# Two multiplies of the decay norm on GpSimd instead of VectorE, from block 3 on

## The chip, the cores and the metric

The kernel runs on one core of a Trainium2 chip. The core has a matrix engine (TensorE, PE in the profile), three engines for elementwise work (VectorE or DVE, ScalarE or ACT, GpSimd or POOL), an engine that issues transfers (SyncE or SP) and 16 DMA engines. Every engine runs its own list of instructions in order and waits on semaphores for the others. The metric is the device time of one execution in microseconds. The kernel before takes 1702.69 us, the median of three runs (1702.55 to 1706.17).

## The reference

A linear attention with complex, data-dependent decays feeds a mixture of eight experts whose gates are balanced by eight Sinkhorn steps. Shapes: batch 4, 8 heads, 768 steps, head size 48; 3072 tokens of 384 features; expert width 1024.

```python
mag = np.sqrt(a_re * a_re + a_im * a_im)
scale = np.minimum(mag, 0.999) / (mag + 1e-06)
a_re_n, a_im_n = (a_re * scale, a_im * scale)
for t in range(S):
    S_re, S_im = decay(S_re, S_im; a_re_n[t], a_im_n[t]) + (k[t] v[t], 0)
    y[t] = q[t] . S_re
x = y as 3072 x 384
P = sinkhorn(exp(x @ w_gate - max), 8 rounds)
out = sum over e of P[:, e] * (relu(x @ w1[e]) @ w2[e])
```

(The loop over t is shortened here.) The change touches the third line alone: the two products of a decay's real and imaginary part with its scale.

## The kernel before

The tokens are cut into 12 blocks of 256 (two batch entries by 128 steps). The first stage, about the first 550 us, goes through the blocks, and for each of them does the following.

- `norm`: loads the decays z (128 partitions, real and imaginary part, 768 columns each), works out the scale on ScalarE and VectorE, and multiplies both parts by it. The factor lies in the tile tx; L438 (L436 in the first two blocks) writes it last, and L440 makes the two products, in place in z. z has two buffers, z_236 and z_237, used by even and odd blocks.
- `scan`: forms the products of the decays over the steps of a chunk, on VectorE (L467 to L473), in place in z.
- `post`: from these the scaled keys kh (L511 to L526) and the scaled queries, in place in z (L530).
- `attention`: SyncE's queue moves kh and z to the tiles ks and qs (L558), TensorE makes the scores (L602), VectorE masks them into sc (L605), TensorE forms the output (L627), and ScalarE and VectorE split it into a high part xh and a low part xl (L642, L643), the x of the block. ScalarE and VectorE also carry the state on (L656 to L666).
- `experts`: experts 0 and 1 on the x of the block before. For each of their 8 column blocks TensorE makes nine matmuls of the first layer (L267 to L269, into ph), ScalarE the relu as hh and hf (L273), VectorE the difference hl (L277), and TensorE six matmuls of the second layer (L285 to L287, into po).

The rest of the time, from about 565 us, TensorE works through experts 2 to 7 by a scheme with fewer products (L1277 to L1279 and L1356 to L1358).

The order of instructions in the first stage is not that of the code. Each piece of work is put down as a job with an engine, a duration that the author supposes, the tiles that it reads and writes, and a rank. `Plan.order` then plays these jobs through: at each point the engine that can start first takes, of its jobs that are ready, the one with the lowest rank. The order that comes out is written into the program for every engine, TensorE's too. So a job's supposed duration moves the instructions of other engines as well. GpSimd had no jobs in this plan; its memsets stand where the code calls for them.

The norm of block i + 1 is put down ahead of the end of block i, and its jobs have ranks that let them run while block i is finished. For the block index i the jobs of L427 to L440 belong to the norm of block i.

Of the kernel before, what the change touches and what calls it, by code (L numbers as in the profile page):

```python
# [10 lines left out]
ALU = mybir.AluOpType  # L11
# [5 lines left out]
E, F = 8, 1024  # L17
# [43 lines left out]
class Plan:  # L61
# [20 lines left out]
    def order(self):  # L82
        n = len(self.ops)
        left = [len(o[5]) for o in self.ops]
        users = [[] for _ in range(n)]
        for k, o in enumerate(self.ops):
            for d in o[5]:
                users[d].append(k)
        ready = [0.0] * n
        self.start, self.end = [None] * n, [None] * n  # L90
        free = {e: 0.0 for e in ("PE", "DVE", "ACT", "SP")}
        queue = {e: [] for e in free}
        for k in range(n):
            if not left[k]:
                queue[self.ops[k][0]].append(k)
        out, pipe = [], 0.0
        while any(queue.values()):
            best = None
            for e, q in queue.items():
                if q:  # L100
                    t = max(free[e], min(ready[k] for k in q))
                    if best is None or t < best[0]:
                        best = (t, e)
            t, e = best
            k = min((k for k in queue[e] if ready[k] <= t + (0.12 if 0 <= self.ops[k][3] < 2000 else 0.35 if -9.6e5 < self.ops[k][3] <= -9e5 else 0.0)), key=lambda k: (self.ops[k][3], k))
            queue[e].remove(k)
            eng, us, run, rank, land, deps, kb, slack = self.ops[k]
            t = max(t, ready[k])
            self.start[k] = t
            free[e] = t + us  # L110
            end = t + (land or us)
            if kb:
                pipe = max(pipe, t + 1.0) + kb / 300.0
                end = max(end, pipe + 1.0)
            self.end[k] = end
            out.append(k)
            for u in users[k]:
                r = end + ((1.2 if self.ops[u][0] == "PE" else 0.2) if land else self.REACH.get((e, self.ops[u][0]), 0.15)) + slack
                ready[u] = max(ready[u], r)
                left[u] -= 1  # L120
                if not left[u]:
                    queue[self.ops[u][0]].append(u)
        assert len(out) == n
        return out


class Net:
# [188 lines left out]
    def phase1(self, c1, ca):  # L316
        tc, nc = self.tc, self.nc
# [68 lines left out]
        self.opening(K)  # L386
        order = self.plan.order()
        n = 1 + max(k for k, o in enumerate(order) if o not in self.expert and o not in self.late)
        assert not self.late & set(order[:n])
        E_ = mybir.EngineType  # L390
        with tc.manual_schedule(engines={E_.DVE, E_.Activation, E_.SP}):
            for k in order[:n]:
                self.plan.ops[k][2]()
        self.rest = [self.plan.ops[k][2] for k in order[n:]]
# [7 lines left out]
    def norm(self, i):  # L402
        nc, V, A, job = self.nc, self.nc.vector, self.nc.scalar, self.plan.add
        s, fl, ns = i % 2, self.fl, self.N // SUB
        zt = self.zt[s]
        zn = [("z", s, a, g) for a in range(2) for g in range(NCT * NCH)]
        R = 1000 * i
        if i == 0:
            for k in (0, 3):
                for a in range(2):  # L410
                    job("SP" if a else "ACT", 0.45, lambda a=a, k=k: (nc.sync if a else nc.scalar).dma_start(zt[:, a, k:k + 3, :CH], self.aqk[0, :, a, k:k + 3]), (), [("z", s, a, g) for g in range(k, k + 3)], -2e6 + k, land=3.0, kb=192)
        else:
            job("SP", 0.45, lambda: nc.sync.dma_start(zt[:, :, :, :CH], self.aqk[i, :, 0:2]), (), zn, -1.82e6 if i == 1 else -1e5, land=8.5, kb=768)
        for k, ps in enumerate([range(3), range(3, 6)] if i == 0 else [range(6)]):
            def nm(*t):
                return [(*t, g) for g in ps]

            n, ga, gb = CH * len(ps), ps[0], ps[-1] + 1
            z, sq = zt[:, :, ga:gb, :CH], self.sq[:, :, ga:gb]
            x, y, zz = (t[:, ga:gb] for t in (self.tx, self.ty, self.tz))  # L420
            zs = [("z", s, a, g) for a in range(2) for g in ps]
            X, Y, Z = nm("tx"), nm("ty"), nm("tz")
            f0, f1 = (i, ns + i) if k == 0 else (2 * ns + ns * NCT * NCH, 2 * ns + ns * NCT * NCH + 1)
            r = R - 1001 if i > 2 else R - 401 if i == 2 else R - 90 if i else R - 300 + 20 * k
            u = 900 if i > 2 else 0
            job("ACT", n / 522 + 0.1, lambda z=z, sq=sq, f0=f0: A.activation(sq, z, AF.Square, accum_out=fl[:, f0:f0 + 1]), zs, Y + Z, r - 5e5)
            job("DVE", n / 960 + 0.105, lambda sq=sq, x=x: V.scalar_tensor_tensor(x, sq[:, 0], 1e-20, sq[:, 1], ALU.max, ALU.add), Y + Z, X, r)  # L427
            job("ACT", n / 1045, lambda x=x, y=y: A.activation(y, x, AF.Abs_reciprocal_sqrt), X, Y, r + 1 - 5e5)
            job("ACT", n / 1045 + 0.1, lambda y=y, zz=zz, f1=f1: A.activation(zz, y, AF.Square, accum_out=fl[:, f1:f1 + 1]), Y, Z, r + 2 - 5e5)
            job("DVE", n / 960 + 0.075, lambda x=x, zz=zz: V.tensor_tensor(x, x, zz, ALU.mult), X + Z, X, r + 0.1)  # L430
            job("DVE", n / 960 + 0.105, lambda x=x, y=y: V.scalar_tensor_tensor(y, x, -3.0, y, ALU.add, ALU.mult), X + Y, Y, r + 4)
            job("ACT", n / 830, lambda y=y, zz=zz: A.activation(zz, y, AF.Square, bias=self.bm05[:, :1], scale=-0.5e-6), Y, Z, r + 5 - 5e5)
            if i < FOLD:
                job("DVE", n / 1920 + 0.087, lambda x=x, y=y: V.tensor_scalar(x, y, -0.4995, 1.0, ALU.mult, ALU.min), Y, X, r + 6)
                job("DVE", n / 960 + 0.105, lambda x=x, zz=zz: V.scalar_tensor_tensor(x, zz, 0.75, x, ALU.add, ALU.mult), X + Z, X, r + 7 + u)
            else:  # L436
                job("ACT", n / 1045, lambda zz=zz: A.activation(zz, zz, AF.Identity, bias=self.bw[:, :1], scale=-0.4995), Z, Z, r + 6 - 5e5)
                job("DVE", n / 960 + 0.105, lambda x=x, y=y, zz=zz: V.scalar_tensor_tensor(x, y, -1 / 0.4995, zz, ALU.max, ALU.mult), Y + Z, X, r + 7 + u)  # L438
            for a in range(2):
                job("DVE", n / 960 + 0.075, lambda z=z, x=x, a=a: V.tensor_tensor(z[:, a], z[:, a], x, ALU.mult), X + zs[a * len(ps):(a + 1) * len(ps)], zs[a * len(ps):(a + 1) * len(ps)], r + 8 + a + u)  # L440

    def scan(self, i):
        V, job = self.nc.vector, self.plan.add
# [1182 lines left out]
```

## Time and profile before

| | |
|---|---|
| median of three runs | 1702.69 us |
| span of the profiled execution | 1699.2 us, 3.5 us less than the median |
| TensorE busy | 1672.3 us (98%) |
| VectorE busy | 1281.3 us (75%) |
| ScalarE busy | 803.1 us (47%) |
| GpSimd busy | 8.9 us (1%) |

The span runs from the first to the last instruction on the core; the execution also has some time around it, which the runs' times hold and the span doesn't. Busy times are unions: two matmuls that overlap in TensorE's pipeline count once. The mean duration of a matmul (334 ns for 384 columns, say) is longer than the distance between two of them, since they overlap. GpSimd's 20 instructions are all memsets.

### The profile page before, as it was taken

To read this page: it belongs to the slowest core of one execution; us is meant where nothing else is said; L and a number is where in the kernel's file an instruction comes from. 1 tells how busy PE (TensorE), PEld (TensorE's weight loads), DVE (VectorE), ACT (ScalarE), POOL (GpSimd) and SP (SyncE) were. 2 spreads that over 40 slices of the span, in tenths; PEclk is the share of its full clock that TensorE was granted. 3 is DMA by queue.
4 is the path that set the end of the run, shared out by engine and by line. 5 is a ranking of instruction groups with operands and counts; after the bars stand their busy time and mean duration, and the time that the engine had idled before them with its cause. 6 is when DMAs were issued, how large, how long until landed. Compare 5 with 4: busy or idle time off the path is not lost.

```text
span 1699.2 us, 35042 instructions
## 1 busy us (share of the span) xinstructions
PE 1672.3 (98%) x13776; PEld 1631.4 (96%) x13776; DVE 1281.3 (75%) x2942; ACT 803.1 (47%) x1866; POOL 8.9 (1%) x20
## 2 busy tenths in 40 slices
PE   6999999999999999999999999999999999999998
PEld 3899999999999999999999999999999999999998
DVE  8899989999994989999854767665566766465665
ACT  7766656656553655555543333333333333333332
POOL 1000000000000000000000000000000000000000
PEclk9999999999999999999999999999999999999999
DMA  7445555445545888788875565666465566555460
GB/s 228 124 116 136 125 131 130 118 118 131 130 105 151 261 320 299 272 277 293 305 263 215 198 229 193 257 239 240 178 224 204 214 250 222 211 193 211 183 245 35
DMA packets 163469, 338.79 MB, mean 199 GB/s; under 512 B 14880, under 2 KB 122848, under 8 KB 163296
## 3 DMA queue, kind: packets, MB, share of 16 engines
q1 hardware_dynamic: 162496, 336.08, 59.0%
q8 instruction: 110, 1.80, 0.4%
q14 instruction: 63, 0.52, 0.1%
q10 hardware_dynamic: 800, 0.39, 0.1%
HBM read 236.27 MB, written 81.20 MB: 187 GB/s over the span
## 4 chain that ended last, share of the span: by engine, by line


## 5 line engine op out<-in xcount | busy, mean ns | idle before, releaser
L1376 ACT ACTIVATE hh<-s 128x384 fp32r<-128x384 f32 x378 | 198.9, 526 | 413.7 <-DVE s L1372 373.2
L1372 DVE TENSOR_TENSOR s<-s,A 128x384 f32<-128x384 f32 x315 | 174.0, 552 | 139.5 <-PE A L1358 137.0
L1279 PE MATMUL po<-w_d,hl 128*128 128x384 f32 x768 | 256.6, 334 | 0.0
L1278 PE MATMUL po<-w_d,hh 128*128 128x384 f32 x768 | 256.6, 334 | 0.0
L1277 PE MATMUL po<-w_d,hh 128*128 128x384 f32 x768 | 256.6, 334 | 0.0
L1383 DVE SCALAR_TENSOR_TENSOR hl<-s,hh 128x384 fp32r<-128x384 f32 x378 | 208.7, 552 | 6.1
L267 PE MATMUL ph<-xh,w 128*128 128x256 f32 x576 | 165.7, 288 | 1.2 <-ACT hl L273 0.8
L269 PE MATMUL ph<-xh,w 128*128 128x256 f32 x576 | 162.3, 282 | 0.0
L268 PE MATMUL ph<-xl,w 128*128 128x256 f32 x576 | 162.2, 282 | 0.0
L1369 ACT ACTIVATE s<-B 128x384 f32<-128x384 f32 x189 | 92.9, 491 | 117.7 <-PE B L1358 114.4
L1372 DVE TENSOR_TENSOR s<-s,B 128x384 f32<-128x384 f32 x189 | 104.1, 551 | 53.9 <-PE B L1358 51.6
L1277 PEld LDWEIGHTS po<-w_d,hh 128*128 128x128 f32 x768 | 144.2, 188 | 0.0
L1278 PEld LDWEIGHTS po<-w_d,hh 128*128 128x128 f32 x768 | 144.2, 188 | 0.0
L1279 PEld LDWEIGHTS po<-w_d,hl 128*128 128x128 f32 x768 | 144.2, 188 | 0.0
L273 ACT ACTIVATE hh<-ph 128x256 fp32r<-128x256 f32 x192 | 73.5, 383 | 131.2 <-PE ph L269 130.7
L285 PE MATMUL po<-w,hh 128*128 128x384 f32 x384 | 131.6, 343 | 0.0
L286 PE MATMUL po<-w,hh 128*128 128x384 f32 x384 | 128.9, 336 | 0.0
L287 PE MATMUL po<-w,hl 128*128 128x384 f32 x384 | 128.8, 336 | 0.0
L1279 PE MATMUL po<-w_c,hl 128*128 128x384 f32 x384 | 128.3, 334 | 0.0
L1278 PE MATMUL po<-w_c,hh 128*128 128x384 f32 x384 | 128.3, 334 | 0.0
L1277 PE MATMUL po<-w_c,hh 128*128 128x384 f32 x384 | 128.3, 334 | 0.0
L1391 DVE TENSOR_TENSOR s<-s,B 128x384 f32<-128x384 f32 x63 | 34.9, 554 | 115.7 <-PE B L1358 115.7
(258 smaller groups left out, 4075.7 us busy)
## 6 DMA issues: line engine op xcount, KB each, us to landing
w_d<-w_d SPq DMA_DIRECT2D x64, 768.0 KB, 7.2
w_a<-w_d SPq DMA_DIRECT2D x48, 768.0 KB, 4.3
w_b<-w_d SPq DMA_DIRECT2D x48, 768.0 KB, 5.7
w_c<-w_d SPq DMA_DIRECT2D x48, 768.0 KB, 6.3
raw<-in_w_dram SPq DMA_DIRECT2D x32, 576.0 KB, 5.8
w_d<-w_a SPq DMA_DIRECT2D x16, 768.0 KB, 3.2
w_d<-w_b SPq DMA_DIRECT2D x16, 768.0 KB, 5.0
w_d<-w_c SPq DMA_DIRECT2D x16, 768.0 KB, 6.3
```

What stands on the lines that cost most here:

```text
L267: nc.tensor.matmul(p, w[:, 0, cs], xh[:, ct, :], start=(ct == 0), stop=False)
L268: nc.tensor.matmul(p, w[:, 0, cs], xl[:, ct, :], start=False, stop=False)
L269: nc.tensor.matmul(p, w[:, 1, cs], xh[:, ct, :], start=False, stop=(ct == NCT - 1))
L285: nc.tensor.matmul(o, hh[:, s], w2h, start=f == 0, stop=False)
L286: nc.tensor.matmul(o, hh[:, s], w2l, start=False, stop=False)
L287: nc.tensor.matmul(o, hl[:, s], w2h, start=False, stop=f == NF - 1)
L1277: nc.tensor.matmul(po[k], hh[:, s], w2[:, 0], start=c == 0, stop=False)
L1278: nc.tensor.matmul(po[k], hh[:, s], w2[:, 1], start=False, stop=False)
L1279: nc.tensor.matmul(po[k], hl[:, s], w2[:, 0], start=False, stop=c == NF - 1)
L1372: V.tensor_tensor(S[nm], S[nm], ps, op)
L1376: A.activation(hh, S[nm], AF.Relu)
L1383: V.scalar_tensor_tensor(hl, S[nm], 0.0, hh.bitcast(F32), ALU.max, ALU.subtract)
```

## The change

For blocks 3 to 11 the two multiplies of L440 become jobs of GpSimd, with a supposed duration of n/400 + 0.2 us, which is 2.12 us for n = 768, in place of n/960 + 0.075. For that the plan gets a fifth engine, and the scheduler of the surrounding framework is told that GpSimd's order is given too. Blocks 0 to 2 stay as they were.

```diff
-        free = {e: 0.0 for e in ("PE", "DVE", "ACT", "SP")}
+        free = {e: 0.0 for e in ("PE", "DVE", "ACT", "SP", "POOL")}
...
-        with tc.manual_schedule(engines={E_.DVE, E_.Activation, E_.SP}):
+        with tc.manual_schedule(engines={E_.DVE, E_.Activation, E_.SP, E_.Pool}):
             for k in order[:n]:
                 self.plan.ops[k][2]()
...
             for a in range(2):
-                job("DVE", n / 960 + 0.075, lambda z=z, x=x, a=a: V.tensor_tensor(z[:, a], z[:, a], x, ALU.mult), X + zs[a * len(ps):(a + 1) * len(ps)], zs[a * len(ps):(a + 1) * len(ps)], r + 8 + a + u)
+                job("POOL" if i > 2 else "DVE", n / 400 + 0.2 if i > 2 else n / 960 + 0.075, lambda z=z, x=x, a=a, E=nc.gpsimd if i > 2 else V: E.tensor_tensor(z[:, a], z[:, a], x, ALU.mult), X + zs[a * len(ps):(a + 1) * len(ps)], zs[a * len(ps):(a + 1) * len(ps)], r + 8 + a + u)
```

The instructions move as follows. On GpSimd the 18 multiplies stand in pairs behind the memsets of block 1 (L631), with one row of another kind ahead of them. The end of its list before, and the same place now:

```order
L631 MEMSET st_222 128x512
L631 MEMSET st_223 128x512
L841 MEMSET lt_8469 128x384
L841 MEMSET lt_8502 128x384
```

```order
L631 MEMSET st_222 128x512
L631 MEMSET st_223 128x512
L440 ISA
L440 TENSOR_TENSOR z_237<-z_237,tx 128x6x128 x2
L440 TENSOR_TENSOR z_236<-z_236,tx 128x6x128 x2
```

Nothing else on GpSimd moved; the other seven pairs follow in the same way, even and odd buffers in turn.

On VectorE the place is the norm of block 10, whose buffer is z_236; hl_8_n are the differences of the experts on block 8, and L530 ends block 9. Before:

```order
L438 SCALAR_TENSOR_TENSOR tx<-sq 128x768
L440 TENSOR_TENSOR z_236<-z_236,tx 128x6x128
L277 TENSOR_TENSOR hl_8_1_6535<-hf_8_1_6517,hh_8_1_6470 128x256
L512 SCALAR_TENSOR_TENSOR ta<-kh 128x768
L277 TENSOR_TENSOR hl_8_2_6554<-hf_8_2_6541,hh_8_2_6537 128x256
L440 TENSOR_TENSOR z_236<-z_236,tx 128x6x128
L517 TENSOR_TENSOR kh<-ta,tb 128x768
```

Now:

```order
L530 TENSOR_TENSOR z_237<-z_237,qk 128x6x128
L438 SCALAR_TENSOR_TENSOR tx<-sq 128x768
L277 TENSOR_TENSOR hl_8_4_6627<-hf_8_4_6624,hh_8_4_6621 128x256
L277 TENSOR_TENSOR hl_8_5_6652<-hf_8_5_6649,hh_8_5_6646 128x256
L467 TENSOR_TENSOR ta<-z_236 128x12x32
L467 TENSOR_TENSOR tb<-z_236 128x12x32
```

The two multiplies are gone from the list, and in this block the factor (L438) stands behind the keys and queries of block 9 and right ahead of the scan of block 10, with two L277 between. In the other blocks it stays ahead of L517, as before.

On TensorE the place is the first scores of block 9 (L602); here the names have their buffer numbers, and w1_3 is expert 1, column block 3. Before:

```order
L285 MATMUL po0_206<-w1_3_430,hh1_8_3_6776 128x384
L286 MATMUL po0_206<-w1_3_430,hh1_8_3_6776 128x384
L287 MATMUL po0_206<-w1_3_430,hl1_8_3_6791 128x384
L285 MATMUL po1_207<-w1_3_430,hh1_8_3_6776 128x384
L286 MATMUL po1_207<-w1_3_430,hh1_8_3_6776 128x384
L287 MATMUL po1_207<-w1_3_430,hl1_8_3_6791 128x384
L602 MATMUL s0_208<-qs_212,ks_213 32x4x8
```

Now:

```order
L287 MATMUL po1_207<-w0_5_324,hl0_8_5_6652 128x384
L267 MATMUL ph0_204<-xh8_6169,w1_0_389 128x256
L268 MATMUL ph0_204<-xl8_6170,w1_0_389 128x256
L269 MATMUL ph0_204<-xh8_6169,w1_0_389 128x256
L267 MATMUL ph0_204<-xh8_6169,w1_0_389 128x256
L268 MATMUL ph0_204<-xl8_6170,w1_0_389 128x256
L269 MATMUL ph0_204<-xh8_6169,w1_0_389 128x256
L267 MATMUL ph0_204<-xh8_6169,w1_0_389 128x256
L268 MATMUL ph0_204<-xl8_6170,w1_0_389 128x256
L269 MATMUL ph0_204<-xh8_6169,w1_0_389 128x256
L602 MATMUL s0_208<-qs_212,ks_213 32x4x8
```

The scores of block 9 now stand behind the first layer of expert 1, column block 0; before they stood behind the second layer of its column block 3. The work in front of them is less, the total is the same.

## Rows read from the trace of the kernel before

**Rows 1.** The page: busy time, share, instructions; busy tenths in 40 slices.

```profile
PE 1672.3 (98%) x13776; PEld 1631.4 (96%) x13776; DVE 1281.3 (75%) x2942; ACT 803.1 (47%) x1866; POOL 8.9 (1%) x20
...
PE   6999999999999999999999999999999999999998
...
DVE  8899989999994989999854767665566766465665
```

**Rows 2.** TensorE's waits, 60 to 1699 us: total us, times, longest.

```profile
PE s L602 <- DMA ye_d<-yst: 1.9, 2, 1.7
PE ph L267 <- ACT hl L273: 0.8, 1, 0.8
PE ph L267 <- ACT hf L273: 0.5, 2, 0.2
PE B L1356 <- DVE s L1372: 0.3, 1, 0.3
```

**Rows 3.** Timeline, TensorE at 262 us: start, length, instruction.

```profile
262.07 0.28 PE L267 MATMUL ph<-xh,w 128*128 128x256 f32 x1
...
262.78 0.34 PE L285 MATMUL po<-w,hh 128*128 128x384 f32 x1
...
263.83 0.28 PE L267 MATMUL ph<-xh,w 128*128 128x256 f32 x1
```

**Rows 4.** Busy time of each engine in 100 to 504 us.

```profile
core 0: us, PE busy (x) PEld busy (x) DVE busy (x) ACT busy (x) POOL busy (x), PEclk, DMA share, GB/s
100.00:504.00 404.00, 401.84 (x5752) 385.16 (x5743) 376.58 (x931) 246.47 (x686) 0.99 (x2) 1.00 0.48 122
```

**Rows 5.** VectorE by line, 100 to 504 us: busy us, mean ns, idle before.

```profile
L605 DVE COPY_PREDICATED sc<-mask,s 128x512 f32<-128x512 uint8 x36 | 25.7, 735 | 3.0 <-PE s L602 3.0
...
L440 DVE TENSOR_TENSOR z<-z,tx 128x768 f32<-128x768 f32 x18 | 17.2, 955 | 0.3
...
L643 DVE TENSOR_TENSOR xl<-yp,xh 128x384 fp32r<-128x384 f32 x19 | 10.6, 556 | 2.8 <-ACT xh L642 2.3
...
L656 DVE TENSOR_TENSOR tm<-st,U 112x384 f32<-112x384 f32 x16 | 8.7, 547 | 0.0
...
L427 DVE SCALAR_TENSOR_TENSOR tx<-sq 128x768 f32<-128x768 f32 x9 | 8.6, 956 | 1.2 <-ACT sq L426 1.2
```

**Rows 6.** VectorE's waits, 100 to 504 us: total us, times, longest.

```profile
DVE hl L277 <- ACT hf L273: 6.7, 13, 1.0
DVE kh L517 <- ACT tb L514: 3.4, 4, 1.0
```

**Rows 7.** Timeline of VectorE: the multiplies of blocks 3 and 6.

```profile
118.34 0.95 DVE L440 TENSOR_TENSOR z<-z,tx 128x768 f32<-128x768 f32 x1
...
293.61 0.96 DVE L438 SCALAR_TENSOR_TENSOR tx<-sq 128x768 f32<-128x768 f32 x1 [0.62 <-ACT sq L437]
294.61 0.96 DVE L440 TENSOR_TENSOR z<-z,tx 128x768 f32<-128x768 f32 x1
295.48 0.95 DVE L517 TENSOR_TENSOR kh<-ta,tb 128x768 f32<-128x768 f32 x1
...
297.89 0.95 DVE L440 TENSOR_TENSOR z<-z,tx 128x768 f32<-128x768 f32 x1
298.76 0.42 DVE L277 TENSOR_TENSOR hl<-hf,hh 128x256 fp32r<-128x256 f32 x1
...
307.87 0.55 DVE L467 TENSOR_TENSOR ta<-z 128x384 f32<-128x384 f32 x1
```

**Rows 8.** GpSimd by line, whole span; then its timeline at 103 us.

```profile
L340 POOL MEMSET qs<- 32x2064 f32 x1 | 1.8, 1810 | 0.3 <-POOLq L1618 0.3
...
L631 POOL MEMSET st<- 128x512 f32 x2 | 1.0, 529 | 95.7 <-PE yp L627 95.7
...
103.48 0.99 POOL L631 MEMSET st<- 128x512 f32 x2 [95.70 <-PE yp L627]
```

**Rows 9.** Timeline of VectorE beside those memsets.

```profile
103.79 0.95 DVE L427 SCALAR_TENSOR_TENSOR tx<-sq 128x768 f32<-128x768 f32 x1
```

**Rows 10.** Timeline of SyncE's queue, ScalarE and TensorE, scores of block 5.

```profile
263.59 3.80 SPq L558 DMA_DIRECT2D qs<-z  x6
...
271.79 0.22 ACT L634 ACTIVATE rr<-qs 48x8 f32<-48x8 f32 x1 [1.81 <-DMA qs<-z]
...
272.38 1.33 PE L602 MATMUL s<-qs,ks 112*32 112x32 f32 x64
```

## The prediction

> **What bounds the kernel now.** I read the busy shares first, then TensorE's waits, then the stretch in which the change lies. TensorE is busy for 98% of the span and in every slice but the first and the last [rows 1]. A busy share alone could hide a stretched matmul, so the second view is its list of waits: from 60 us to the end it names 3.5 us in all, the longest 1.7 us [rows 2]. The third is the spacing: six matmuls of an expert's first layer start within 0.71 us and six of the second within 1.05 us, one close behind the other [rows 3]. So TensorE has no slack to give back. A microsecond that it is made to wait in the attention stage is added to the end, since nothing later is idle that could take it up; and no relief of another engine can be worth more than about 3.5 us. VectorE is the engine next to it: between 100 and 504 us, which holds all but the first and last blocks, it is busy 376.58 of 404 us [rows 4].
>
> **What is removed.** Blocks 3 to 11 each lose two VectorE multiplies of 128x768; the stretch has all 18 of them [rows 5]. One lasts 0.95 us, but the next instruction starts 0.87 us behind its start (294.61 to 295.48 and 297.89 to 298.76 us) [rows 7]. VectorE is freed of 2 x 0.87 = 1.74 us in a block, 15.7 us in all.
>
> **What GpSimd's multiply lasts.** The trace has only its memsets: 0.53 us for 512 columns and 1.81 us for 2064, that is 0.82 ns for a column beside 0.11 us fixed [rows 8]. A multiply of 768 columns writes once and reads twice. If reading hides behind writing it takes 0.63 + 0.11 = 0.74 us, if all three passes follow each other 3 x 0.63 + 0.11 = 2.0 us; with the write hidden behind two reads it is 1.37 us. I take 1.7, the middle of the last two, and keep 0.74 and 2.0. The extra GpSimd row that stands ahead of its first multiply comes right behind two memsets that start at 103.48 us [rows 8]; VectorE reached that multiply at 118.34 [rows 7], so I cost it at nothing.
>
> **What VectorE pays beside it.** No row shows GpSimd reading SBUF beside VectorE. While GpSimd only wrote, VectorE's neighbours kept their length: 0.95 us for the 128x768 form at 103.79 us, whose mean is 0.956 [rows 5, 9]. That clears writing and says nothing on reading. The ends are: not held at all, or held for the whole multiply whenever its own instruction reads both inputs from SBUF. Three groups read one input from PSUM (the scores' masked copy, the low part of x, the state's sum): 25.7 + 10.6 + 8.7 = 45.0 us [rows 5]. The rest, 376.6 - 45.0 = 331.6 us, is 82% of the stretch. A full hold therefore costs 2 x 1.7 x 0.82 = 2.8 us in a block against 1.74 saved: VectorE becomes 1.05 us slower per block, not faster.
>
> **What the planner makes of it.** TensorE's order is fixed when the program is built, and it now believes that VectorE is faster. Ahead of the first scores of block 9 there stood 142 first-layer and 140 second-layer groups of the experts, now 137 and 134, counted in the whole order (the piece in front moves from expert 1, column block 3 of block 8 to the start of expert 1). By [rows 3] a first-layer group of nine matmuls takes 1.065 us, a second-layer group of six 1.05. TensorE asks for these scores 5 x 1.065 + 6 x 1.05 = 11.6 us earlier. How late may they be? The transfers of qs had landed by 271.79 us, when ScalarE began on them, and the scores started at 272.38: 0.6 us [rows 10].
>
> **The sum.** Seven pairs (blocks 3 to 9) are multiplied before the scores of block 9: 7 x 1.05 = 7.4 us of VectorE. Lateness there is 7.4 + 11.6 - 0.6 = 18.4 us. A late VectorE saves the waits that it now spends on ScalarE's output of the experts, 6.7 us [rows 6]; the other waits (3.4 us on the chain of the keys and smaller ones) follow VectorE's own results and stay. That leaves 11.7, say 12 us, on TensorE. Block 9 is where the order has moved most: at block 11 it is 9 x 1.05 + 6.4 (four and two groups) - 0.6 - 6.7 = 8.6, already paid. In block 10 the order puts the factor (L438) just ahead of the scan, with two L277 between; there GpSimd's pair stands open before the scan, at most 3.4 us once, against 1.74 saved and in place of a hold; I count it like the others. What is late next is TensorE's scores and, behind them, the first expert matmuls on a new x.
>
> The profiled span is 1699.2 us and the median of the runs 1702.69, 3.5 us above it; what is added inside the span is added to both. Forecast: 1702.7 + 12 = 1714.7 us.
>
> **What decides.** With no hold VectorE gains 7 x 1.74 = 12.2 us up to the scores of block 9, which the order's 11.6 has already spent. With 0.6 us of slack and 6.7 of reclaimed waits, 7.9 us over 14 multiplies may be lost, 0.56 us each. That is less than the shortest that a multiply can last. So any hold over a third of a 1.7 us multiply shows in the time, and it is this that makes slower likelier than the same.
>
> A page speaks against the change. The Trainium skill (SBUF — State Buffer, "Who interferes with whom") says that a VectorE instruction with two SBUF inputs and a GpSimd instruction that reads SBUF share a read interface, and that the one that comes second waits until the first is done. No run here shows it yet; the memset beside L427 fits its exception for instructions that only write. By that rule the time is the forecast's. Another page (GPSIMD Engine Reference, "Performance versus the Vector engine") measures 4497 ns for an add of 2048 columns; an estimate from it is 1.69 us for 768, and the sum by it would be the same 12 us.
>
> **Rivals.** First, no hold: the engines read side by side. For it speaks the memset at 103.5 us, against it that a memset reads nothing. The gain of 12.2 us and the earlier order cancel, TensorE waits no more than now, and of its 3.5 us of waits some may go: 1700 to 1703 us, 1702 as its middle, which is the same. Chance 0.22. It decides where a multiply costs VectorE less than 0.56 us.
>
> Second, half a hold, each slowing the other: 1.4 us in a block against 1.74, so 7 x -0.34 = -2.4, and -2.4 + 11.6 - 0.6 - 6.7 = 2 us, 1704.6. Chance 0.09, mostly the same.
>
> Third, a long multiply: GpSimd is turned away by VectorE's back-to-back instructions, or is slow itself, and the pair ends after the scan is due. At 2.5 us, over the dearest row bound, with a full hold, 2 x 2.5 x 0.82 - 1.74 = 2.4 in a block, 16.5 + 11.6 - 7.3 = 21 us, 1723.5; more where the scan waits in every block. Against it: in block 6 the factor is ready at 294.57 us and the scan starts at 307.87 [rows 7], 13.3 us for a pair that needs 3.4. Chance 0.07.
>
> Last, faster by more than the bound: all the 3.5 us of waits go and something in the opening with them. Nothing in TensorE's rows has room for it. Chance 0.04.
>
> **Numbers.** The forecast has 0.58. Its own ends: at 0.74 us and a full hold 2 x 0.74 x 0.82 - 1.74 = -0.53 in a block, -3.7 + 11.6 - 7.3 = 0.6 us, no loss; at 2.0 us 1.54 in a block, 10.8 + 11.6 - 7.3 = 15; with the hold charged to all of VectorE's time 2.26, 15.8 + 4.3 = 20. The range, 1701 to 1722, takes in the first two rivals and leaves out most of the third and the last. About 0.2% (3.4 us) is what a measurement of this kernel can tell from no change. Slower: 0.58 + 0.07 + 0.02 of the half hold = 0.67. Same: 0.22 + 0.07 = 0.29. Faster: 0.04.
>
> **What would show it.** In the new profile GpSimd should have 18 multiplies of 1.4 to 2.0 us between about 115 and 480 us. Beside them single VectorE instructions of a known size should be 1 to 2 us longer, or start that much later with no releaser named. VectorE's busy time in 100 to 504 us should not fall by 15 us. TensorE should show new waits of 1 to 2 us each, on qs transfers before L602 and on x before L267, 10 to 14 us in sum, most in blocks 4 to 9, and none behind 560 us. I am wrong if VectorE's instructions beside a multiply keep their length, or if TensorE's waits stay at 3 to 4 us, or if the added time lies behind the attention stage.

## The result, and the profile after

The changed kernel takes 1.0101 times the time of the one before (95% interval 1.0089 to 1.0113), 17 us more. Its runs have a median of 1720.28 us (1717.19 to 1721.9); with a fourth run beside them, the kernel before has 1704.04 us. The forecast was 12 us more, 1714.7 us.

The page after, the lines that answer to [rows 1]: busy time, and the busy tenths of the 40 slices.

```profile
PE 1677.2 (98%) x13776; PEld 1634.8 (95%) x13776; DVE 1289.5 (75%) x2924; ACT 803.1 (47%) x1866; POOL 45.7 (3%) x38
...
PE   6999999999999999999999999999999999999998
...
POOL 1010010001000000000000000000000000000000
```

VectorE has 18 instructions less and is busy for 8 us more. GpSimd has grown from 8.9 to 45.7 us. TensorE's busy digits don't show the loss: a slice is 43 us wide, and a wait of 2 us leaves a 9 in it. The waits show it. TensorE's, 60 to 1719 us, as in [rows 2]: total, times, longest.

```profile
PE ph L267 <- ACT hf L273: 3.6, 3, 1.7
PE s L602 <- issue: 3.4, 1, 3.4
PE s L602 <- DMA ye_d<-yst: 2.8, 4, 1.4
PE s L602 <- DMA qs<-z: 2.0, 2, 1.1
PE yp L627 <- issue: 0.9, 2, 0.6
...
PE po L287 <- DVE hl L277: 0.5, 2, 0.3
```

With three small ones the list sums to 15.1 us, where it was 3.5. Nearly all stand at the scores (L602), at the output that follows them (L627) and at the experts' matmuls that wait for a relu or for hl. The releaser "issue" says only that the profile shows none. Where the longest stands (until 366.28 us), the transfers of qs are the likely cause: the last of the six was issued at 360.4 us, and they took 4.4 to 5.6 us to land.

VectorE by line, 100 to 504 us before and 100 to 518 us after (the same 9, 16 or 18 instructions of each line of the norm and the keys): busy us, mean ns, idle before. The kernel before first.

```profile
L277 DVE TENSOR_TENSOR hl<-hf,hh 128x256 fp32r<-128x256 f32 x143 | 59.6, 420 | 8.0 <-ACT hf L273 6.7
...
L666 DVE TENSOR_TENSOR st<-sa,sb 112x384 f32<-112x384 f32 x18 | 9.9, 551 | 0.0
L664 DVE TENSOR_TENSOR sb<-tm,qs 48x384 f32<-48x384 f32 x16 | 8.9, 554 | 0.5
...
L517 DVE TENSOR_TENSOR kh<-ta,tb 128x768 f32<-128x768 f32 x9 | 8.6, 955 | 3.4 <-ACT tb L514 3.4
L512 DVE SCALAR_TENSOR_TENSOR ta<-kh 128x768 f32<-128x768 f32 x9 | 8.6, 955 | 1.1 <-ACT kh L511 1.1
```

The changed kernel:

```profile
L277 DVE TENSOR_TENSOR hl<-hf,hh 128x256 fp32r<-128x256 f32 x140 | 69.1, 498 | 11.6 <-ACT hf L273 10.9
...
L517 DVE TENSOR_TENSOR kh<-ta,tb 128x768 f32<-128x768 f32 x9 | 12.8, 1420 | 5.0 <-ACT tb L514 4.9
L666 DVE TENSOR_TENSOR st<-sa,sb 112x384 f32<-112x384 f32 x18 | 12.7, 706 | 0.0
L512 DVE SCALAR_TENSOR_TENSOR ta<-kh 128x768 f32<-128x768 f32 x9 | 11.6, 1284 | 0.3 <-ACT kh L511 0.2
...
L664 DVE TENSOR_TENSOR sb<-tm,qs 48x384 f32<-48x384 f32 x16 | 10.2, 638 | 0.5
```

The same instructions on the same shapes are longer, and the increase stands in the five lines that run beside a multiply: 69.1 - 140 x 0.42 = 10.3 us in L277, and 4.2, 2.8, 3.0 and 1.3 us in the four others, 21.6 us in all or 1.2 us for each of the 18 multiplies. An instruction that reads one input from PSUM is not held. L665 reads U from there in block 3, lies wholly inside the first multiply, and keeps its 0.55 us:

```profile
118.30 3.54 POOL L440 TENSOR_TENSOR z<-z,tx 128x768 f32<-128x768 f32 x2 [11.27 <-DVE tx L438]
```

```profile
118.82 0.55 DVE L665 TENSOR_TENSOR sb<-U,rn 48x384 f32<-48x384 f32 x1
```

How that looks in time, block 6: GpSimd's pair, and VectorE beside it.

```profile
295.31 4.18 POOL L440 TENSOR_TENSOR z<-z,tx 128x768 f32<-128x768 f32 x2 [40.17 <-DVE tx L438]
```

```profile
295.15 0.95 DVE L512 SCALAR_TENSOR_TENSOR ta<-kh 128x768 f32<-128x768 f32 x1
296.02 1.97 DVE L277 TENSOR_TENSOR hl<-hf,hh 128x256 fp32r<-128x256 f32 x1
298.02 2.30 DVE L517 TENSOR_TENSOR kh<-ta,tb 128x768 f32<-128x768 f32 x1
300.24 0.41 DVE L277 TENSOR_TENSOR hl<-hf,hh 128x256 fp32r<-128x256 f32 x1
```

L512 came first and kept its length; the pair takes 4.18 us here and 3.54 in block 3, so the first multiply waited for it. Then L277 was held behind the first multiply (1.97 us where 0.42 is due) and L517 behind the second (2.30 for 0.95). The two engines take turns, an instruction at a time.

Behind the attention stage hardly anything changed: in 900 to 1500 us TensorE is busy for over 199.8 of each 200 us, as before.

### The profile page after: what moved, and what is told of

It is laid out like the page before. It is cut to its first block, busy times and chain, and to the rows that moved or that the text cites. A ratio compares the mean times of both kernels' runs of the same rounds, so it can differ in the third digit from the quotient of the medians.

```text
span 1718.6 us, 35079 instructions
## 1 busy us (share of the span) xinstructions
PE 1677.2 (98%) x13776; PEld 1634.8 (95%) x13776; DVE 1289.5 (75%) x2924; ACT 803.1 (47%) x1866; POOL 45.7 (3%) x38
## 4 chain that ended last, share of the span: by engine, by line
## 5 line engine op out<-in xcount | busy, mean ns | idle before, releaser
L267 PE MATMUL ph<-xh,w 128*128 128x256 f32 x576 | 165.5, 287 | 4.4 <-ACT hf L273 3.6
L287 PE MATMUL po<-w,hl 128*128 128x384 f32 x384 | 129.1, 336 | 0.5 <-DVE hl L277 0.5
```

What stands on the lines that cost most here:

```text
L267: nc.tensor.matmul(p, w[:, 0, cs], xh[:, ct, :], start=(ct == 0), stop=False)
L287: nc.tensor.matmul(o, hl[:, s], w2h, start=False, stop=f == NF - 1)
```

## The experiments

Each kernel differs from the changed one in the job of L440 alone. Times are given as ratios to the kernel before, run on the same chip, with the 95% interval; 0.001 is 1.7 us. Another number is used to see where the time lies: the distance from the first L267 of one block to that of the next on TensorE's timeline, the last one to the start of the last L287 (in us, worked out from the start times of these matmuls; the blocks are those of the experts):

```
block              0     1     2     3     4     5     6     7     8     9    10    11    sum
before            47.1  45.1  43.1  46.7  45.9  43.6  45.9  43.6  45.9  44.2  39.8  43.5  534.5
after             47.5  46.6  44.9  48.0  46.9  46.8  49.5  47.1  44.6  42.6  41.3  44.4  550.1
e1 order kept     47.7  46.6  45.4  46.8  45.9  44.7  46.0  44.3  46.0  45.2  39.9  43.5  541.9
e2 order only     47.3  46.0  43.4  47.2  46.8  46.8  46.2  46.3  44.8  41.6  41.3  43.6  541.5
e3 write only     47.3  44.9  42.8  46.8  45.6  46.3  45.8  45.0  44.7  41.7  41.7  44.4  537.1
e4 hold of 1.5    47.3  47.6  48.6  45.7  44.7  45.4  46.5  46.4  44.8  44.2  40.9  43.5  545.7
e5 relief only    47.4  44.8  43.0  46.3  45.9  43.6  45.9  43.6  45.9  44.2  39.8  43.5  534.0
e6 one multiply   47.6  45.1  46.3  48.9  46.9  43.7  46.6  43.6  46.7  44.3  39.9  43.5  543.0
e7 one input      47.1  46.0  43.4  47.3  46.3  43.6  46.2  43.6  46.2  44.2  39.8  43.5  537.3
e8 hold of 1.2    47.7  47.2  45.7  44.8  44.6  44.6  45.2  44.6  44.9  44.2  40.3  43.5  537.3
e9 blocks 3, 4    47.6  46.6  45.3  45.9  45.9  43.6  45.9  43.6  45.9  44.2  39.8  43.5  537.8
e10 from block 5  47.7  44.8  43.2  46.5  45.9  44.7  45.9  44.3  46.1  45.1  39.8  43.5  537.7
```

The two profiled executions differ by 19.4 us (1718.6 - 1699.2). Of these, 15.6 lie in this stretch (550.1 - 534.5) and 1.6 behind it. The other 2.2 lie ahead of it, before any of the changed work: the first L267 comes at 58.8 us before and at 61.0 after, and anywhere up to 63.6 us in the experiments.

**The multiplies on GpSimd, the order of before (e1).**

```diff
-job("POOL" if i > 2 else "DVE", n / 400 + 0.2 if i > 2 else n / 960 + 0.075, lambda ...
+job("DVE", n / 960 + 0.075, lambda ...
```

> The 18 multiplies run on GpSimd, but the plan still counts them as VectorE's, so every other engine keeps the order of the kernel before. Theory (hold and order add up, and share one slack): VectorE is held about 1.2 us per multiply, as the trace after shows (69.1 us of L277 where 140 x 0.42 = 58.8 were due, and 1.3 to 4.2 us more in L512, L517, L664, L666: 21.6 us over 18 multiplies), against 0.87 saved, so some 0.7 us later per block, 6 us at block 11; slack of 0.6 us and the waits for the relu take it up: 0 to +4 us over before. Rival, the hold alone: the full +17 us. Rival, the order alone: -3 to 0 us.

Measured: 1.0049 (1.0036 to 1.0063), 8.3 us. Neither the theory's +4 nor the rival's +17. TensorE's waits, 60 to 600 us; before, L602 had 1.9 us, L267 0.5 in the second line, and L287 none:

```profile
PE s L602 <- DMA ye_d<-yst: 4.0, 3, 1.9
PE ph L267 <- ACT hf L273: 2.0, 2, 1.7
PE po L287 <- DVE hl L277: 1.4, 4, 0.4
```

The hold by itself makes half of the loss. The slack that the sum had put against it was hardly there: VectorE still waited 7.4 us for the relu in 100 to 518 us.

**The order of the changed kernel, the multiplies on VectorE (e2).**

```diff
-lambda z=z, x=x, a=a, E=nc.gpsimd if i > 2 else V: E.tensor_tensor(...
+lambda z=z, x=x, a=a: V.tensor_tensor(...
```

> Plan and order of the changed kernel, but the multiplies are issued by VectorE, at the places that the plan gave them: nothing reads on GpSimd. Theory: TensorE asks for the scores of block 9 up to 11.6 us earlier while VectorE does all the work that it did before; less 0.6 us of slack and up to 6.7 us of reclaimed waits: +4 to +11 us. Rival, the hold alone: 0 us, within 2. Rival, the order alone: the full +17 us.

Measured: 1.0047 (1.0034 to 1.0061), 8.0 us, as the theory had it. No VectorE instruction is longer (L277 has a mean of 420 ns), and TensorE's waits, 60 to 600 us, are at other places than in the run before:

```profile
PE ph L267 <- ACT hf L273: 2.2, 3, 1.1
PE yp L627 <- issue: 1.9, 2, 1.6
PE s L602 <- DMA qs<-z: 1.5, 1, 1.5
PE s L602 <- issue: 1.3, 1, 1.3
```

8.3 + 8.0 = 16.3, against 17.2 for both: the two terms of the sum are there, of about the same size, and within the noise (each interval is some 2.3 us to either side) they add up. Block by block they don't quite: blocks 1 and 2 lose by the hold (e1), blocks 5 and 7 by the order (e2), and the 3.6 us of block 6 are in neither alone (0.1 and 0.3 us) but in both together.

**The order of the changed kernel, memsets for the multiplies (e3).**

```diff
+lambda z=z, x=x, a=a: nc.gpsimd.memset(z[:, a], 0.1 if a else 0.9) if i > 2 else V.tensor_tensor(...
```

> As the changed kernel, but GpSimd's multiplies are memsets of the same z (0.9 and 0.1 in place of the products, so blocks 3 to 11 do without the scale and the decays): GpSimd writes beside VectorE and reads nothing. Theory: no hold, VectorE gains 1.74 us a block, which the earlier order spends: -2 to +3 us over before, and L277, L512, L517, L666 keep their mean lengths of before. Rival, any work of GpSimd holds VectorE: L277 and the others stay longer by 0.7 us for each memset, +8 us or more.

Measured: 1.0018 (1.0008 to 1.0028), 3.1 us, the upper end of the theory. GpSimd beside VectorE, and VectorE beside it:

```profile
188.58 1.41 POOL L440 MEMSET z<- 128x768 f32 x2 [39.28 <-ACT sq L426]
```

```profile
188.46 0.49 DVE L470 TENSOR_TENSOR tb<-z 128x126 f32<-128x126 f32 x2
188.99 0.29 DVE L471 TENSOR_TENSOR z<-ta,tb 128x126 f32<-128x126 f32 x1
...
189.39 0.95 DVE L427 SCALAR_TENSOR_TENSOR tx<-sq 128x768 f32<-128x768 f32 x1
```

Writing holds nothing: all keep their lengths. A memset doesn't need the factor, so it starts earlier than a multiply, as soon as ScalarE has read z (L426), and it is shorter; but the multiply of e7 (below) starts at the same event, reads, and does lengthen VectorE's instructions. So it is reading beside VectorE that costs. And this is close to the first rival of the prediction made real: a GpSimd that takes the work without a hold. It gives no gain either; the earlier order spends all of it and 3 us more (blocks 5 and 7 are 2.7 and 1.4 us longer than before).

**Memsets, the order of before (e5).** The edits of e1 and e3 together.

> Memsets of z by GpSimd in place of the multiplies of blocks 3 to 11 (0.9 and 0.1 for the products, so scale and decays are left out there), and the order of the kernel before on every other engine. VectorE loses 15.7 us of work and is not held. Theory, TensorE bounds and its work is unchanged: 0 us, within 3, over before, TensorE's waits stay at 1 to 4 us. Rival, VectorE bounds: -8 to -16 us.

Measured: 1.0004 (0.9992 to 1.0015), the same. VectorE had 15.7 us less to do and TensorE's expert stretch shrank by 0.5 us. VectorE spent the rest on waiting, 100 to 518 us (4.6 us before in the first line, 7.0 in the second):

```profile
DVE kh L517 <- ACT tb L514: 12.6, 9, 2.3
DVE hl L277 <- ACT hf L273: 8.3, 21, 0.9
```

So TensorE bounds, and relief of VectorE is worth nothing here in the order of before. That another order would turn the relief into a gain was not tried; TensorE's list of waits before, 3.5 us in all [rows 2], is what could be won back.

**A plan that charges VectorE for the hold (e4, e8).** The multiplies on GpSimd, 1.5 us and then 1.2 us of VectorE counted for each.

```diff
+job("DVE", n / 960 + 0.7 if i > 2 else n / 960 + 0.075, lambda ...
+job("DVE", n / 960 + 0.4 if i > 2 else n / 960 + 0.075, lambda ...
```

> The multiplies run on GpSimd, and the plan counts 1.5 us of VectorE for each (0.8 us in the kernel before), so TensorE's order comes later than before instead of earlier. Theory: the attention work is asked for about when it is there, TensorE's waits from 60 us on fall from 15 to 3 to 8 us: 0 to +6 us over before. Rival, the hold alone: the waits stay, +17 us.

> As the run in which the plan counted 1.5 us of VectorE for each multiply, with 1.2 us, which is the hold that the trace shows (22.3 us over 18). Theory A, a plan with the true cost fits best: +5 to +8 us, under the run that kept the order (+8.3). Theory B, every later placing of TensorE's attention work costs, since VectorE then waits for the scores (6.1 us on L605 with 1.5 us counted, 3.0 before): between that run and the one with 1.5 us, +8 to +12 us.

Measured: 1.0070 (1.0056 to 1.0084), 12 us, with 1.5; 1.0016 (1.0006 to 1.0026), 2.7 us, with 1.2. The first lies between its theory and the rival, and TensorE's waits are 10.1 us where 3 to 8 were expected; a later order is not a safe one, and this one cost more than the order of before. The second is better than both theories: the plan that counts the measured hold loses a third of what the order of before loses with the same multiplies. That this is because the cost is true is not shown; 0.8, 1.2 and 1.5 us are three orders, of which one fits. TensorE's waits at the scores are almost gone, 1.3 us in all (60 to 1720 us):

```profile
PE ph L267 <- ACT hf L273: 2.5, 2, 1.7
PE ph L267 <- ACT hl L273: 0.8, 1, 0.8
PE s L602 <- DVE sc L605: 0.7, 3, 0.3
...
PE s L602 <- DMA ye_d<-yst: 0.6, 1, 0.6
```

Why 1.5 us is so much worse than 1.2 was not taken apart. The table puts most of it into blocks 1 and 2 (2.5 and 5.5 us); one part is a wait of 2.11 us at the scores, behind which the granted clock stood at 0.50 from 189.1 to 192.4 us (what that costs is told with the next run).

**One of the two multiplies (e6).** The order of before, GpSimd for the second product alone.

> As the run that kept the order, but only the second product of a block is GpSimd's, the first stays with VectorE: half of the hold, half of the relief. Theory, each multiply costs VectorE its hold less 0.87 us and this goes to the end without slack: half of 8.3, +3 to +5 us. Rival, a slack takes up the first part (as the 6.7 us of reclaimed waits in the sum before): -1 to +1 us.

Measured: 1.0052 (1.0039 to 1.0065), 8.9 us: as dear as both, which neither theory allowed. The blocks show where: 3.2, 2.2 and 1.0 us in blocks 2 to 4, then nothing to 0.8. TensorE waited at the scores for 1.95 us until 185.75 and for 2.30 us until 234.59, and behind each wait its clock fell; busy time and granted clock (the column after POOL) of four stretches:

```profile
183.00:185.60 2.60, 0.79 (x7) 0.59 (x5) 1.51 (x7) 0.43 (x2) 0.00 (x0) 1.00 1.08 306
187.00:190.40 3.40, 3.40 (x45) 2.90 (x38) 3.26 (x13) 0.14 (x1) 0.00 (x0) 0.52 0.80 230
230.00:234.00 4.00, 2.29 (x17) 2.08 (x15) 3.79 (x15) 0.66 (x3) 0.00 (x0) 1.00 1.15 229
234.80:238.20 3.40, 3.40 (x67) 3.34 (x60) 2.22 (x6) 1.06 (x5) 0.00 (x0) 0.52 0.95 308
```

For 3.4 us each the clock stood at 1.2 in place of 2.4 GHz, about 1.7 us of work lost on top of each wait (an estimate, half of the 3.4 us). In the run with both multiplies (e1) the waits at the same scores were a little shorter, 1.88 and 1.69 us, and no such stretch followed. So a loss is not proportional to the hold: behind two of these waits nearly as much again was lost to the clock.

**The place of the hold (e9, e10).** The order of before, GpSimd in blocks 3 and 4 alone, and from block 5 on.

> The order of the kernel before, and GpSimd's multiplies in blocks 3 and 4 alone, VectorE's elsewhere. Theory, the hold is paid where TensorE has no slack, which in the run that kept the order was at the scores and first expert matmuls of blocks 3 and 4 (2 to 2.3 us a block, then 0 to 1.1): +3 to +5 us. Rival, every held multiply costs the same: 2 of 9 blocks, 1.8 of 8.3 us, +1 to +2.5 us.

> The order of the kernel before, and GpSimd's multiplies from block 5 on. Theory, the places without slack are mostly spared, +2 to +4 us. Rival, every held multiply costs the same: 7 of 9 blocks, 6.5 of 8.3 us, +5.5 to +7.5 us.

Measured: 1.0019 (1.0008 to 1.0030), 3.2 us, for two blocks; 1.0016 (1.0006 to 1.0026), 2.7 us, for the other seven. Both lie in the theory's ranges, at the low end: 1.6 us a block against 0.4. The second excludes its rival; the first alone would not, since its interval begins at 1.4 us and the rival's range ends at 2.5. The table agrees: with blocks 3 and 4 alone TensorE loses 1.5 and 2.2 us in its blocks 1 and 2, and from block 4 on its blocks are as long as before (45.9 and 43.6 us). So a held multiply costs by its place more than by its count. That the place is one where TensorE has no slack fits these runs and is argued.

**One input in place of two (e7).** The order of before, GpSimd multiplying z by 1.0.

> As the run that kept the order, but GpSimd multiplies z by the constant 1.0, with one input (so the scale is left out in blocks 3 to 11): it reads one stream in place of two. Theory, reading holds, and as long as GpSimd's instruction lasts: a multiply of some 0.8 us, VectorE's neighbours 0.4 to 0.8 us longer, which its saved 0.87 us covers: -1 to +2 us. Rival, only a second input holds: no VectorE instruction gets longer, -2 to +1 us. Rival, the hold doesn't depend on the multiply's length: +8 us as with two inputs.

Measured: 1.0024 (1.0014 to 1.0034), 4.1 us, outside all three. The premise was wrong: the instruction is not shorter but longer, 2.2 to 2.9 us with its waits. It doesn't read the factor, so it also starts earlier, beside other VectorE instructions than in e1. The pair, and VectorE beside it:

```profile
419.22 5.25 POOL L440 TENSOR_SCALAR z<-z 128x768 f32<-128x768 f32 x2 [40.98 <-ACT sq L426]
```

```profile
419.17 0.96 DVE L427 SCALAR_TENSOR_TENSOR tx<-sq 128x768 f32<-128x768 f32 x1 [0.30 <-ACT sq L426]
420.05 1.05 DVE L277 TENSOR_TENSOR hl<-hf,hh 128x256 fp32r<-128x256 f32 x1
421.02 0.54 DVE L643 TENSOR_TENSOR xl<-yp,xh 128x384 fp32r<-128x384 f32 x1
421.49 0.99 DVE L470 TENSOR_TENSOR tb<-z 128x372 f32<-128x372 f32 x2
422.51 1.05 DVE L471 TENSOR_TENSOR z<-ta,tb 128x372 f32<-128x372 f32 x1
```

One VectorE instruction per multiply is held, by some 0.5 to 0.6 us (L277 1.05 for 0.42, L471 1.05 for 0.54), a quarter of GpSimd's instruction; the two L470 between them, with two SBUF inputs, keep their 0.54 us each. VectorE saved more than that, and yet TensorE lost 2.8 us in the expert stretch. How a hold that is repaid within the block still costs was not settled.

## Why the prediction was right, and where its sum was not

**TensorE bounds.** Right: relief alone changes nothing (e5), and the loss is for the most part TensorE's waiting in the attention stage. Its list of waits grew by 11.6 us, the clock (below) adds 1.7, and some 2 of the 15.6 us stand in neither. Of the waits none came behind 560 us but 0.8 us at L1356.

**The multiply, 1.7 us.** Right: 1.74 and 1.83 us in the shortest pairs (3.53 us), 2.1 us on average with its own waits for VectorE.

**The hold, 1.39 us a multiply.** Right in kind, somewhat large: 1.2 us. Net of the 0.87 us saved that is 0.66 us a block in place of 1.05. It is the rule of the Trainium skill (SBUF — State Buffer, "Who interferes with whom"), and the runs bear it out in three points: an instruction with two SBUF inputs waits (L277, 1.97 us for 0.42), one with a PSUM input doesn't (L665, 0.55 us inside a multiply; in e4 L656, 0.54), a GpSimd instruction that only writes (e3) holds nothing. The section's words "for the whole instruction" are said of another case, VectorE's two-port modes; the two-input multiply behaves as they say, the one-input form (e7) doesn't, with a hold of a quarter of the instruction.

**The order, 11.6 us earlier.** Right in kind: with nothing held it cost 8.0 us (e2), where 11.6 less the 0.6 of slack is 11.0, and 3.1 with the relief that the plan had counted on (e3).

**The reclaimed waits, 6.7 us.** This step failed; its 6.7 us are more than the 5 us by which the forecast is short. The sum took it that a late VectorE would no longer wait for the experts' relu. Those waits grew instead, from 6.7 us [rows 6] to 10.9 over the same work (100 to 504 us before, 100 to 518 after), and all of VectorE's listed waits together from 19.6 to 21.8. A likely reason is that with TensorE held up at the scores, the first layer behind them, its relu and so hl come later too: the wait of VectorE for TensorE is not there to be reclaimed when TensorE itself waits. This is argued; in e8 the same waits are 18.1 us although TensorE hardly waits at the scores. Without that term and with the measured hold the sum is 7 x 0.66 + 11.6 - 0.6 = 15.6 us, the 15.6 us of the expert stretch. That this fits is luck: its two parts would be 4.6 us for the hold and 11.0 for the order, and the runs that have one of them alone give 8.3 (e1) and 8.0 us (e2).

**One lateness, paid once.** The sum took the worst place (block 9) and held the rest to be paid by it. The table shows the loss in blocks 1 to 7, 3.2, 3.6 and 3.5 us in blocks 5 to 7, 1.3 and 1.6 us given back in blocks 8 and 9, and 1.5 and 0.9 us more in blocks 10 and 11, which the sum had as already paid. So there is no single worst place, and most of the loss comes before block 9.

**The clock.** It was in no term. In block 6 TensorE stood idle for 3.35 us before the scores, and its clock then fell: busy time and granted clock of two stretches, and the timeline with the matmuls that followed.

```profile
362.90:366.28 3.38, 0.03 (x1) 0.03 (x1) 2.33 (x10) 0.66 (x4) 0.00 (x0) 1.00 1.09 253
...
367.40:370.80 3.40, 3.40 (x59) 3.11 (x52) 2.13 (x6) 1.35 (x5) 0.00 (x0) 0.55 0.98 280
```

```profile
366.28 1.75 PE L602 MATMUL s<-qs,ks 112*32 112x32 f32 x64 [3.35 <-issue]
367.96 0.58 PE L267 MATMUL ph<-xh,w 128*128 128x256 f32 x1
...
370.18 0.88 PE L602 MATMUL s<-qs,ks 112*32 112x32 f32 x32
```

Nine matmuls of the first layer took 370.18 - 367.96 = 2.2 us, where 1.065 are usual [rows 3]. So the longest wait cost 3.35 + 1.7 us, the second figure an estimate: half of the 3.4 us at half clock.

**Block 10.** As costed: the pair ended at 451.45 us, and the scan began at 451.66; TensorE did not wait there (busy for all of 447 to 452 us).

## What to carry to other kernels

Price an elementwise job that goes to GpSimd as the hold that it lays on VectorE less the VectorE time that it saves: here 1.2 against 0.87 us, so it is no relief as long as VectorE reads two SBUF inputs most of the time. Where a planner writes the order of all engines, a job that it books wrongly (here as no work of VectorE at all) is a second change of its own, as dear as the first (8.0 beside 8.3 us), and the same edit with the measured hold in the plan lost 2.7 us in place of 17. And ask first whether the relieved engine bounds at all: here relief alone changed nothing.

## What was not expected of the hardware

- GpSimd's one-input multiply of 128x768 takes at least 2.2 us (2.2 to 2.9 with its waits), longer than the two-input one at 1.74 to 1.83 us, but holds VectorE for some 0.6 us only.
- After single waits of TensorE of 1.95 and 2.30 us (e6), 2.11 (e4) and 3.35 (the changed kernel) its clock stood at 1.2 GHz for 3.4 us each time; after waits of 1.88 and 1.69 us (e1) it stayed at 2.4 GHz. One such stretch costs about 1.7 us, by the estimate with e6.
